# Seven-product first projection for two of six block pairs in token tiles 3 to 6, in the four PSUM banks of the projection's ring

## The chip, the core and the metric

The kernel runs on one core of one Trainium2 chip. The metric is the device time of one execution in microseconds. The engines of the core are called PE (TensorE; PEld is its weight load), DVE (VectorE), ACT (ScalarE), POOL (GpSimd) and SP (SyncE, which only issues transfers here).

## What is computed

Sparse attention over 8 batches, 8 heads, 576 positions and head size 64, followed by a bilinear feed-forward layer over the 4608 tokens. The first four heads see the last 32 positions, the other four see every 32nd position.

```
scores = where(mask, q @ k.T / 8, -1e9);  attn = softmax(scores) @ v
x = attn.transpose(0, 2, 1, 3).reshape(4608, 512)
out = ((x @ w_a) * (x @ w_b)) @ w_out        # 512 -> 1536 -> 512
```

## The kernel before, in words

The work after the start is nine tiles of 512 tokens (t = 0 to 8). A tile is 16 slots that are written out in this order: slots 0 to 11 make one block f of 128 hidden features each (`ffn_ab`, L615), slots 12 to 15 the second projection (`ffn_ys`, L860). A scheduled slot ends with `take(i)`, which puts in the attention steps of a later batch, and with what `do(i, ...)` has put there. All engines follow this written order; nothing is reordered.

**A plain block.** PE multiplies x (bf16, transposed, `xT`) by four 128-row pieces of `wa_sb` into one PSUM bank and by four of `wb_sb` into another (L612): eight products of 128x512. ACT copies the first bank to `a_sb` (L633), DVE multiplies it by the second bank into `pf` (L636). The banks come from `mm_bank` (L598), a ring of four: three of pool "mm" and one of pool "tp". A block takes two. The other four banks belong to the attention: "st" (scores) two, "o" (outputs) two.

**A pair by seven products.** In tiles 7 and 8, where attention is over, `a_pair` (L667) makes two blocks f = 2g and 2g+1 at once: of the two-by-two blocks of w_a and x (two halves of the 512 inputs; two halves of 256 tokens) it forms seven products instead of eight, each two matmuls of 128x256. They are called 1, 6, 7, 2, 5, 4, 3 in its plan (L683). They need sums of weights (`wsum_make`, L648, tiles `wsum_a`) and of inputs (`xsum_make`, L659, tiles `xsum`). Product 1, then 6, then 5 accumulate in bank X, 3 later too, and X is copied out by ACT after each; 7 and 4 accumulate in bank Z; 2 goes to bank Y. DVE adds Y and the second content of Z to the copies, POOL the first content of Z. X, Y and Z lie in three different banks, X in one that the attention has left.

**What else stands in a slot of tiles 3 to 6** (`LATER`, L575, the batch b = t+1). The step after the named slot is, for PE: slot 0 S1, slot 1 V0, slot 2 S2, slot 3 V1, slot 4 S3, slot 5 V2, slot 6 S4, slot 7 V3. S is a score step: PE `st` (L377), ACT exp (L397), DVE mask (L415). V0 to V3 are output steps: PE `o` (L454), DVE reciprocal `rc` (L462) and multiplication `xl` (L480). Q2 after slot 1 and Q3 after slot 3 are two POOL copies each (`step_Q`, L333). `fast_s` (L750) makes sums for the second projection on DVE after slots 4 to 10. `pace` (L1054) is a one-element POOL copy of a slot's result that holds POOL's transfers back until that slot; it stands at each slot in which `do` has put something.

In the tables the step "mask" is L415, "rc" L462, "xl" L480, "ps" L750.

Of the kernel before, what the change touches and what calls it, by code (L numbers as in the profile page):

```python
# [7 lines left out]
F32 = mybir.dt.float32  # L8
BF16 = mybir.dt.bfloat16
I16 = mybir.dt.int16  # L10
ALU = mybir.AluOpType
# [5 lines left out]
RS = 8  # L17
NP = 72
GP = 80
# [5 lines left out]
VW = 128  # L25
WCH = (0, 2, 5, 9, 12)
FAST_Y = (1, 2, 3, 4, 5, 6, 7, 8)
FAST_A = {7: (1, 2, 3, 4, 5), 8: (0, 1, 2, 3, 4, 5)}


@with_exitstack
def kernel(
# [10 lines left out]
    nc = tc.nc  # L43
    B, H, S, D = q.shape
# [5 lines left out]
    KD = d_model // 128  # L50
    FD = d_ff // 128
    TTOK = 512
    NT = n_tok // TTOK
# [3 lines left out]
    const = ctx.enter_context(tc.tile_pool(name="const", bufs=1))  # L57
    wp = ctx.enter_context(tc.tile_pool(name="weights", bufs=1))
    nat = ctx.enter_context(tc.tile_pool(name="nat", bufs=1))
    sb = ctx.enter_context(tc.tile_pool(name="sb", bufs=3))  # L60
    fsb = ctx.enter_context(tc.tile_pool(name="ffn", bufs=2))
# [18 lines left out]
    qz_flat = [[l.rearrange("p a b c -> p (a b c)"), s.rearrange("p a b c d -> p (a b c d)")] for l, s in qz_pair]  # L80
# [3 lines left out]
    vl_buf = [const.tile([128, HL * 6, VW], BF16, name=f"vl{i}") for i in range(2)]  # L84
# [75 lines left out]
    XR = 4  # L160
    xT = const.tile([128, KD, XR * S], BF16)
    wa_sb = wp.tile([128, KD, d_ff], BF16)
    wb_sb = wp.tile([128, KD, d_ff], BF16)
    wo_sb = wp.tile([128, FD, d_model], BF16)

    FG = FD // 2
    HT = TTOK // 2
# [9 lines left out]

    tl = {}

    def blocks(nm, z):  # L180
        z = int(z)
        return sb.tile([128, 2, (S, RS * GP)[z]], BF16, tag=f"t{nm}{z}", name=f"t{nm}{z}", bufs=1)


    nats = {}
# [408 lines left out]
    pfs = {}  # L594
# [3 lines left out]
    def mm_bank(shape):  # L598
        nm = "tp" if used[0] % 4 == 3 and used[0] >= 0 else "mm"
        used[0] += 1  # L600
        return psum4[nm].tile(shape, F32, tag=nm, name="mm")
# [13 lines left out]
    def ffn_ab(t, f, mid, ab=None):  # L615
        if f == 0:
            pfs[t] = fsb.tile([128, FD, TTOK], BF16, tag="pf", name="pf", bufs=1)
        pf = pfs[t]
        if f // 2 in FAST_A.get(t, ()):
            if f % 2 == 0:  # L620
                pairs[t, f // 2] = a_pair(t, f // 2)
            return next(pairs[t, f // 2])
        if ab is None:
            ab = [mm_bank([128, TTOK]) for _ in range(2)]
            if f == 0:

                late = 1 if t == 1 else 3
                for kks in ((0, 2, 3), (1,)) if t == 1 else ((0, 2), (1,), (3,)):
                    ab_mm(t, f, ab, kks, last=kks[-1] if kks[-1] == late else -1)
            else:  # L630
                ab_mm(t, f, ab, range(KD), mid)
        a_sb = fsb.tile([128, TTOK], F32, tag="a_sb", name="a_sb")
        nc.scalar.copy(a_sb, ab[0])  # L633
        if t in FAST_Y:
            halves = lambda x: x.rearrange("p (a i s) -> p a i s", i=2, s=16)
            nc.vector.tensor_mul(pf[:, f, :].rearrange("p (i a s) -> p a i s", i=2, s=16), halves(a_sb), halves(ab[1]))  # L636
        else:
            nc.vector.tensor_mul(pf[:, f, :], a_sb, ab[1])
        return pf[:1, f, :1]

    wav = wa_sb.rearrange("p (j c) (g e m) -> p j c g e m", c=2, e=2, m=128)
    wsum_a = [flat.rearrange("p (c g m) -> p c g m", c=2, g=FG)
              for flat in [vl_buf[0].rearrange("p a b -> p (a b)")[:, 12 * 128 * z:12 * 128 * (z + 1)] for z in range(2)]
              + [t[:, :12 * 128] for t in qz_flat[0]]]
    xsum = {t: qz_flat[1][t - 7][:, :8 * HT].rearrange("p (n c m) -> p n c m", n=4, c=2)
            for t in FAST_A}

    def wsum_make(n):  # L648
        w, s_ = (lambda e, j: wav[:, j, :, :, e]), wsum_a
        a, b, op = ((w(1, 0), w(1, 1), ALU.add), (s_[0], w(0, 0), ALU.subtract), (w(0, 0), w(1, 0), ALU.subtract),  # L650
                    (w(0, 1), s_[1], ALU.subtract))[n]
        for c in range(2):
            nc.vector.tensor_tensor(s_[n][:, c], a[:, c], b[:, c], op=op)

    def x_part(t, j, k):
        x0 = TTOK * t % (XR * S) + HT * k
        return xT[:, 2 * j:2 * j + 2, x0:x0 + HT]

    def xsum_make(t, n):  # L659
# [4 lines left out]

    pairs = {}

    def a_pair(t, g):  # L667

        pf = pfs[t]
        pool, nm = ((pst, "st"), (psum4["o"], "o"))[g % 2]  # L670
        X = pool.tile([128, 2, 512], F32, tag=nm, name="ax")[:, 0, :HT]
        a = ([fsb.tile([128, TTOK], F32, tag="a_sb", name="a_sb") for _ in range(2)] if g % 2 == 0 else
             [t.rearrange("p h n -> p (h n)")[:, :2 * TTOK].bitcast(F32) for t in kT_buf[0]])
        got = {k: psum4[nm].tile([128, TTOK], F32, tag=nm, name="mm")
               for k, nm in zip((1, "Z", "Y", 0), (("mm", "mm", "tp", "mm"), ("tp", "mm", "mm", "mm"))[g % 2])}
        Z, Y = got["Z"][:, :HT], got["Y"][:, :HT]
        p7 = fsb.tile([128, HT], F32, tag="p7", name="p7")
        quarter = lambda e, k: a[e][:, HT * k:HT * (k + 1)]
        w = lambda e, j: (lambda c: wav[:, j, c, g, e])
        ws = lambda n: (lambda c: wsum_a[n][:, c, g])  # L680
        x = lambda j, k: (lambda c: x_part(t, j, k)[:, c])
        xs = lambda n: (lambda c: xsum[t][:, n, c])
        plan = {"1": (X, w(0, 0), x(0, 0)), "2": (Y, w(0, 1), x(1, 0)), "3": (X, ws(3), x(1, 1)), "4": (Z, w(1, 1), xs(3)),  # L683
                "5": (X, ws(0), xs(0)), "6": (X, ws(1), xs(1)), "7": (Z, ws(2), xs(2))}

        def P(k):
            bank, lhs, rhs = plan[k]
            for c in range(2):
                nc.tensor.matmul(bank, lhsT=lhs(c), rhs=rhs(c), start=k in "172" and c == 0, stop=c == 1, skip_group_check=True)  # L689

        x0 = TTOK * t % (XR * S)

        def b_mm(e, kks):
            f = 2 * g + e
            for kk in kks:
                nc.tensor.matmul(got[e], lhsT=wb_sb[:, kk, 128 * f:128 * (f + 1)], rhs=xT[:, kk, x0:x0 + TTOK],  # L696
                                 start=kk == 0, stop=kk == KD - 1)

        def mult(e):
            halves = lambda v_: v_.rearrange("p (a i s) -> p a i s", i=2, s=16)  # L700
            nc.vector.tensor_mul(pf[:, 2 * g + e, :].rearrange("p (i a s) -> p a i s", i=2, s=16),
                                 halves(a[e]), halves(got[e]))

        P("1")
        nc.scalar.copy(quarter(0, 0), X)
        b_mm(1, (0, 1, 2))
        P("6")
        nc.scalar.copy(quarter(1, 0), X)
        b_mm(1, (3,))
        P("7")  # L710
        nc.scalar.copy(p7, Z)
        P("2")
        nc.vector.tensor_tensor(quarter(0, 0), Y, quarter(0, 0), op=ALU.add)
        yield None
        P("5")
        nc.scalar.copy(quarter(1, 1), X)
        nc.gpsimd.tensor_tensor(quarter(1, 1), quarter(1, 1), p7, op=ALU.add)
        if (t, g - 1) in later:
            later.pop((t, g - 1))()
        b_mm(0, (0, 1))  # L720
        P("4")
        nc.vector.tensor_tensor(quarter(1, 0), Z, quarter(1, 0), op=ALU.add)
        P("3")
        nc.scalar.copy(quarter(0, 1), X)
        b_mm(0, (2, 3))
        if g < FG - 1:
            mult(1)
            mult(0)
        else:
            mult(0)  # L730
            if t < NT - 1:
                fast_s(t, 2, slice(4, 6))
            mult(1)
        yield pf[:1, 2 * g + 1, :1]
# [172 lines left out]
    with tc.manual_schedule(engines={ENG.PE, ENG.SP, ENG.Pool, ENG.DVE, ENG.Activation}):  # L907
# [30 lines left out]
        for nm in ORDER:  # L938
            if nm[0] == "*":
                spin(int(nm[1:]))  # L940
            elif nm == "C0":
                for x, cp, n in ((raw[0], nc.vector.tensor_copy, "k"), (raw[1], nc.scalar.copy, "q")):
                    t = nats[0, n, False][:, 0:2].rearrange("p h r d -> p (h r d)")
# [21 lines left out]
            elif nm[0] == "F":  # L965
                f = int(nm[1])
# [6 lines left out]
                elif nm == "F0B":  # L973
                    first[f].append(psum4["o"].tile([128, 512], F32, tag="o", name="ab"))
                ab_mm(0, f, first[f], {"A": (0, 1), "B": (0, 1), "b": (2,), "c": (3,)}[nm[2]],
                      ws={"A": (0,), "B": (1,)}.get(nm[2], (0, 1)))
# [5 lines left out]
        for t in range(NT):  # L982
            slots += [(ffn_ab, t, f) for f in range(FD)] + [(ffn_ys if t in FAST_Y else ffn_y, t, j) for j in range(4)]
        for b in range(1, B):
# [8 lines left out]
        def do(i, fn, *args):  # L993
            at.setdefault(i, []).append(lambda: fn(*args))

        soon = {}
        for t in FAST_Y[:-1]:
            if t not in FAST_A:
# [21 lines left out]
            for (z, nm), g in zip(((0, "k"), (0, "q"), (1, "k"), (1, "q")), gs):  # L1020
                do(g0 + g, step_D, b, z, nm)
        for n in range(4):
            do(16 * (NT - 3) + 2 * n + 2, wsum_make, n)
        do(16 * (NT - 2) - 1, xsum_make, NT - 2, 0)
        for n in (2, 1, 3):
            do(16 * (NT - 2), xsum_make, NT - 2, n)
# [11 lines left out]
        for g in range(FG):  # L1038
            for n in range(4):
                do(16 * (NT - 1) + 2 * g + 1, fast_s, NT - 1, n, slice(g, g + 1))  # L1040
        for t in FAST_Y[:-1]:
            for slot, n, z0, z1 in ((4, 0, 0, 2), (5, 2, 0, 2), (6, 1, 0, 2), (7, 3, 0, 2), (8, 2, 2, 4), (9, 0, 2, 4),
# [45 lines left out]
```

## Time and profile before

| what | value |
|---|---|
| three timed runs | 326.03, 326.70, 327.37 us (median 326.7) |
| the profiled execution | 326.64 us; its span is 324.9 us |
| granted TensorE clock | 0.997 |
| PE busy | 315.5 us, 97% of the span |
| DVE, ACT, POOL busy | 234.1, 186.4, 150.1 us |
| tile 3 / 4 / 5 / 6, first product of slot 0 | 127.97 / 161.64 / 195.55 / 229.22 us |

Times in the profile are counted from the start of the span. A row of the timeline gives start, duration, engine, source line, operation, destination and sources, and in brackets how long the engine was idle before and for whom. A matmul row of four products of 128x512 lasts 1.03 us to the last value in PSUM, but the next one starts 0.862 us after it, since matmuls overlap; spacing is therefore taken from starts. The same holds for DVE rows that follow each other.

### The profile page before, as it was taken

What the parts mean: (1) busy time and instruction counts of PE and PEld (TensorE: products, weight loads), DVE (VectorE), ACT (ScalarE), POOL (GpSimd) and SP (SyncE); (2) the same over time, 40 slices, a digit from 0 to 9 for tenths busy, and PEclk for the clock granted to TensorE, in tenths of its full rate; (3) what the DMA queues carried; (4) which work ended last, traced back from release to release, by engine and by line L of the source; (5) the groups of instructions that cost most, each with busy time, mean ns of one, the idle gap of its engine ahead of it and who ended that gap; (6) DMA issues with size and microseconds to landing.
All of it is one profiled execution on the core that took longest, in us unless ns stands there. A gap on an engine that the chain in (4) does not pass through costs nothing.

```text
span 324.9 us, 7111 instructions
## 1 busy us (share of the span) xinstructions
PE 315.5 (97%) x2706; PEld 214.2 (66%) x2734; DVE 234.1 (72%) x489; ACT 186.4 (57%) x331; POOL 150.1 (46%) x240
## 2 busy tenths in 40 slices
PE   8999999998999999999999999999999999999994
PEld 6754555454765578556999995559555866786684
DVE  6765786498956785688667766777699667857862
ACT  6763766454754476447644765467546655535541
POOL 8944922893785356524652565336124003202520
PEclk9999999999999999999999999999999999999998
DMA  8999999999699999999998999999863030004004
GB/s 150 155 204 196 204 187 204 204 126 175 87 132 153 191 129 101 131 207 167 102 104 181 158 107 107 158 182 112 59 101 103 2 113 17 3 2 129 0 3 129
DMA packets 127234, 40.40 MB, mean 124 GB/s; under 512 B 115040, under 2 KB 124320, under 8 KB 127008
## 3 DMA queue, kind: packets, MB, share of 16 engines
q0 software_dynamic: 80400, 19.28, 64.5%
q1 hardware_dynamic: 46656, 20.61, 36.3%
q8 instruction: 21, 0.34, 0.5%
q14 instruction: 13, 0.11, 0.1%
q10 hardware_dynamic: 144, 0.07, 0.1%
HBM read 39.12 MB, written 18.28 MB: 177 GB/s over the span
## 4 chain that ended last, share of the span: by engine, by line
PE 89%; DVE 4%; ACT 2%; issue 2%; DMA 2%; POOL 0%; ACTq 0%; POOLq 0%
PE mm L612 42%; PE mm L816 18%; PE mm L696 5%; PE st L377 4%; PE mm L878 3%; PE ax L689 3%; PE o L454 2%; PE mm L689 2%; PE o L513 2%; DMA shared<-in_q_dram 2%; PE mm L843 2%; PE end L843 1%; DVE p L415 1%; PE misc L156 1%; PE tp L540 1%
## 5 line engine op out<-in xcount | busy, mean ns | idle before, releaser
L612 PE MATMUL mm<-xT,wb_sb 128*128 128x512 bf16 (+1 forms) x381 | 88.0, 352 | 0.4
L612 PE MATMUL mm<-xT,wa_sb 128*128 128x512 bf16 (+1 forms) x367 | 86.6, 351 | 0.6
L633 ACT COPY a_sb<-mm 128x512 f32<-128x512 f32 x84 | 49.2, 585 | 47.1 <-PE mm L612 45.5
L636 DVE TENSOR_TENSOR pf<-a_sb,mm 128x512 bf16<-128x512 f32 x74 | 50.6, 684 | 26.0 <-PE mm L612 18.4
L612 PEld LDWEIGHTS <-wb_sb 128*128 128x128 bf16 x392 | 37.8, 98 | 33.7 <-issue 0.4
L1054 POOL CAST pace<-pf 1x1 f32<-1x1 bf16 x72 | 21.0, 291 | 77.0 <-DVE pf L636 47.8
L612 PEld LDWEIGHTS <-wa_sb 128*128 128x128 bf16 x392 | 34.9, 98 | 20.9
L397 ACT ACTIVATE p<-st 72x576 bf16<-72x576 f32 (+1 forms) x56 | 36.4, 650 | 20.1 <-PE st L377 19.8
L816 PEld LDWEIGHTS <-ps 128*128 128x128 bf16 x336 | 32.5, 98 | 4.6 <-issue 0.5
L527 DVE TENSOR_TENSOR xT<-o,xr 64x576 bf16<-64x576 f32 x24 | 18.0, 751 | 19.8 <-ACT xr L524 19.6
L816 PE MATMUL mm<-wf,ps 128*128 128x256 bf16 x252 | 30.1, 273 | 0.5 <-ACT y_sb L781 0.3
L781 ACT COPY y_sb<-mm 128x512 f32<-128x512 f32 (+1 forms) x32 | 17.9, 559 | 19.3 <-PE mm L816 16.6
L816 PEld LDWEIGHTS <-pf 128*128 128x128 bf16 x252 | 23.6, 98 | 2.7
L696 PE MATMUL mm<-xT,wb_sb 128*128 128x512 bf16 x83 | 25.3, 379 | 0.1
L816 PE MATMUL mm<-wo_sb,pf 128*128 128x256 bf16 x168 | 21.8, 273 | 0.0
L750 DVE TENSOR_TENSOR ps<-pf 128x512 bf16<-128x512 bf16 (+1 forms) x49 | 21.2, 433 | 0.7
L523 ACT ACTIVATE xr<-o 64x576 f32<-64x576 f32 x24 | 15.6, 648 | 9.4 <-PE o L513 9.2
L1054 POOL COPY pace<-y_sb 1x1 f32<-1x1 f32 x17 | 4.1, 241 | 36.0 <-ACT y_sb L887 13.3
L236 POOL DMA_DIRECT2D vs<-in_v_dram x24 | 20.4, 863 | 0.0
L415 DVE TENSOR_TENSOR p<-p,mask_s 72x576 int16<-72x576 int16 x28 | 18.7, 669 | 1.8 <-ACT p L397 1.5
L454 PEld LDWEIGHTS <-p 128*128 128x128 bf16 (+1 forms) x256 | 13.0, 97 | 8.9 <-DVE xl L480 2.1
L415 DVE TENSOR_TENSOR p<-p,mask_l 128x576 int16<-128x576 int16 x32 | 14.7, 458 | 4.3 <-ACT p L397 4.3
(183 smaller groups left out, 546.7 us busy)
## 6 DMA issues: line engine op xcount, KB each, us to landing
out_dram<-y_sb SPq DMA_DIRECT2D x14, 512.0 KB, 4.9
kr<-in_k_dram POOLq DMA_DIRECT2D x12, 288.0 KB, 5.8
qr<-in_q_dram POOLq DMA_DIRECT2D x12, 288.0 KB, 6.9
vl<-in_v_dram POOLq DMA_DIRECT2D x6, 384.0 KB, 9.5
out_dram<-y_sb SPq DMA_DIRECT2D x7, 256.0 KB, 4.1
vs<-in_v_dram POOLq DMA_DIRECT2D x24, 72.0 KB, 5.9
xd<-xl SPq DMA_DIRECT2D x12, 144.0 KB, 4.8
wo_sb<-in_moe_w_out_dram POOLq DMA_DIRECT2D x4, 384.0 KB, 10.4
```

Of the source, the lines that this page charges most:

```text
L236: nc.gpsimd.dma_start(out=vs_buf[b % 2][:, h, :, 0:D], in_=v[b, HL + h].rearrange("(p r) d -> p r d", r=RS))
L397: nc.scalar.activation(p_flat(p)[:M, :2 * W].rearrange("p (i n) -> p i n", n=2 * n), st[:M].rearrange("p a (i n) -> p (a i) n", n=256)[:, ...
L415: nc.vector.tensor_tensor(pi, pi, mk, op=ALU.bitwise_and)
L454: nc.tensor.matmul(of[:, j, i, :w], lhsT=pt, rhs=vt, start=True, stop=True)
L527: nc.vector.tensor_mul(dst.rearrange("d (p i j) -> d p i j", i=G, j=2), o[:64, :, :W].rearrange("d j (i p) -> d p i j", p=NP), r)
L612: nc.tensor.matmul(ps_[:, c0:c0 + n], lhsT=w[:, kk, 128 * f:128 * (f + 1)], rhs=xT[:, kk, x0:x0 + n], start=(kk == first and c0 == 0), sto ...
L633: nc.scalar.copy(a_sb, ab[0])
L636: nc.vector.tensor_mul(pf[:, f, :].rearrange("p (i a s) -> p a i s", i=2, s=16), halves(a_sb), halves(ab[1]))
L696: nc.tensor.matmul(got[e], lhsT=wb_sb[:, kk, 128 * f:128 * (f + 1)], rhs=xT[:, kk, x0:x0 + TTOK], start=kk == 0, stop=kk == KD - 1)
L750: nc.vector.tensor_tensor(s[:, n], a, b, op=op)
L816: nc.tensor.matmul(bank[b][:, q], lhsT=lhs(g, q), rhs=rhs(g), start=k in "172" and q == 0 and g == 0, stop=g == FG - 1, skip_group_check=True)
L1054: nc.gpsimd.tensor_copy(pace, done)
```

## The change

- A table `MID_A` names pairs g = 1 and g = 3 (slots 2 and 3, slots 6 and 7) of tiles 3, 4, 5 and 6. They are made by a new function, `a_pair_mid`, instead of as two plain blocks each.
- `a_pair_mid` takes four banks of the ring: X, b1, b0 and one bank YZ, whose first half is Y and whose second half is Z.
- The weights' sums move from the tile before 7 to tile 2 (slots 3, 7, 9 and 13), and lie in staging tiles of the first two batches, which are made larger for this. Each mid tile gets four `xsum_make`: one at the last slot of the tile before, three after its slot 0. They share one buffer, `xsum_mid`.
- `a_sb` has three buffers instead of two.

```diff
+MID_A = {t: (1, 3) for t in (3, 4, 5, 6)}
...
-        if f // 2 in FAST_A.get(t, ()):
+        if f // 2 in FAST_A.get(t, ()) + MID_A.get(t, ()):
             if f % 2 == 0:
-                pairs[t, f // 2] = a_pair(t, f // 2)
+                pairs[t, f // 2] = (a_pair_mid if t in MID_A else a_pair)(t, f // 2)
             return next(pairs[t, f // 2])
...
+    def a_pair_mid(t, g):
...
+        YZ, X, b1, b0 = [mm_bank([128, TTOK]) for _ in range(4)]
+        X, Y, Z = X[:, :HT], YZ[:, :HT], YZ[:, HT:]
+        a = [fsb.tile([128, TTOK], F32, tag="a_sb", name="a_sb", bufs=3) for _ in range(2)]
...
+        P(X, w(0, 0), x(0, 0), True)
+        nc.scalar.copy(quarter(0, 0), X)
+        P(Y, w(0, 1), x(1, 0), True)
+        add(quarter(0, 0), Y)
+        b_mm(b1, 1, (0, 1, 2))
+        P(X, ws(1), xs(1))
+        nc.scalar.copy(quarter(1, 0), X)
+        P(Z, ws(2), xs(2))
+        b_mm(b1, 1, (3,))
+        P(X, ws(0), xs(0))
+        nc.scalar.copy(quarter(1, 1), X)
+        add(quarter(1, 1), Z)
+        yield a[1][:1, HT:HT + 1]
+        b_mm(b0, 0, (0, 1, 2))
+        P(Z, w(1, 1), xs(3))
+        add(quarter(1, 0), Z)
+        b_mm(b0, 0, (3,))
+        P(X, ws(3), x(1, 1))
+        nc.scalar.copy(quarter(0, 1), X)
+        mult(1, b1)
+        mult(0, b0)
+        yield pf[:1, 2 * g, :1]
...
         for n in range(4):
-            do(16 * (NT - 3) + 2 * n + 2, wsum_make, n)
+            do(16 * 2 + (3, 7, 9, 13)[n], wsum_make, n)
+        for t in MID_A:
+            do(16 * t - 1, xsum_make, t, 0)
+            for n in (1, 2, 3):
+                do(16 * t, xsum_make, t, n)
```

`P` is two matmuls of 128x256 into the named half bank, `add` a DVE addition of a half bank to a quarter of `a_sb`, `mult` the multiplication of L701, `b_mm` products of 128x512 with `wb_sb`. By the numbers of `a_pair` the order is 1, 2, 6, 7, 5, then (after the slot's attention step) 4, 3. With the waits that the built program carries, product 7 waits for the addition of Y, product 4 for the addition of Z, products 6, 5 and 3 for the copy of X before them, and the next block's two banks for the last addition of Z and the last copy of X.

## The prediction

> **What bounds the kernel now.** I read the page's first part, then the busy times by stretch (tiles 3, 4 and 5: length, then busy us of PE, PEld, DVE, ACT, POOL), then the timeline of tile 5 and of a pair of tile 7.
>
> ```profile
> PE 315.5 (97%) x2706; PEld 214.2 (66%) x2734; DVE 234.1 (72%) x489; ACT 186.4 (57%) x331; POOL 150.1 (46%) x240
> ```
>
> ```profile
> 128.00:161.60 33.60, 33.44 (x263) 21.35 (x264) 24.43 (x47) 20.12 (x34) 16.85 (x28) 1.00 1.33 156
> 161.60:195.50 33.90, 33.90 (x363) 30.76 (x361) 24.48 (x47) 20.18 (x33) 17.48 (x28) 1.00 1.14 135
> 195.50:229.20 33.70, 33.54 (x264) 21.44 (x265) 24.52 (x47) 20.22 (x34) 15.78 (x26) 1.00 1.38 137
> ```
>
> PE is never idle in the tiles that change, so every matmul removed there is worth its full spacing, and every wait put on PE costs its full length. DVE has room on average (24.5 of 33.7 us). What counts is when DVE is free. Tile 5 around the start of slot 2:
>
> ```profile
> 198.39 1.03 PE L612 MATMUL mm<-xT,wb_sb 128*128 128x512 bf16 x4
> 198.49 0.45 DVE L415 TENSOR_TENSOR p<-p,mask_l 128x576 int16<-128x576 int16 x1
> ...
> 199.20 1.32 POOL L333 COPY qz0s<-qTs 64x576 bf16<-64x576 bf16 x2 [1.34 <-DMA qTs<-qr]
> 199.25 0.35 PE L454 MATMUL o<-vl,p 128*128 128x65 bf16 x6
> 199.44 1.02 PE L612 MATMUL mm<-xT,wa_sb 128*128 128x512 bf16 x4
> 199.53 0.69 DVE L636 TENSOR_TENSOR pf<-a_sb,mm 128x512 bf16<-128x512 f32 x1 [0.59 <-PE mm L612]
> 200.13 0.18 DVE L462 RECIPROCAL rc<-o 96x6 f32<-96x6 f32 x1
> 200.30 1.03 PE L612 MATMUL mm<-xT,wb_sb 128*128 128x512 bf16 x4
> 200.35 0.55 DVE L480 TENSOR_TENSOR xl<-o,rc 96x384 bf16<-96x384 f32 x1
> ```
>
> When PE starts slot 2 (199.44), DVE has just begun the block before (mult, 199.53) and has rc and xl of V0 behind it. Four products of 128x512 take 199.44 to 200.30 on PE, 0.2155 each. The two-matmul products of tile 7 show the other spacings and releases:
>
> ```profile
> 266.97 0.38 PE L689 MATMUL ax<-qz1l,vl 128*128 128x256 bf16 x2
> ...
> 267.39 0.37 ACT L708 COPY kT0s<-ax 128x256 f32<-128x256 f32 x1 [0.49 <-PE ax L689]
> ...
> 268.49 0.38 PE L689 MATMUL mm<-qz1l,wa_sb 128*128 128x256 bf16 x2
> ...
> 268.98 0.42 DVE L722 TENSOR_TENSOR kT0s<-mm,kT0s 128x256 f32<-128x256 f32 x1 [0.44 <-PE mm L689]
> ```
>
> A product's first matmul to its ACT copy is 0.42, the copy 0.37; to its DVE addition 0.49, the addition 0.425. Pairs start at 269.36 and 272.61 there: 3.25 us without a wait.
>
> **The change, part by part.**
>
> *Matmuls.* A pair of plain blocks is 16 x 0.2155 = 3.45 us of PE, the new one 3.25: 0.20 saved, 8 x 0.20 = **1.6 us**.
>
> *Product 7 waits for the addition of Y.* Y and Z share a bank, so 7 may start only when DVE has read Y. In `a_pair` they lie apart, and no row of before shows this wait; it is worked out from rows. Let T be the start of the pair. Products 1, 2, three of b1 and 6 take 3 x 0.218 + 0.647 = 1.30, so PE is at 7 at T+1.30. DVE, in pair g = 1: the mask starts at T-0.95 (198.49) and is out of the way at T-0.54 (mask to next operation 0.41); then come the three new `xsum_make`, spaced 0.38 (the three rows of the same kind in tile 7 fill 265.58 to 266.71), to T+0.59; mult 0.60, rc 0.22, xl 0.47 (208.12 to 208.59), to T+1.88; the addition 0.425, to T+2.31; DVE to PE 0.06 (xl ended at 74.12, the PE row that had waited for it starts at 74.18). Product 7 starts at T+2.36: **1.06 us of PE idle**. In pair g = 3 there is no `xsum_make`, but a `ps` of slot 5: mult starts at T+0.09, the chain 0.60 + 0.22 + 0.47 + 0.38 ends at T+1.76, the addition at T+2.19, product 7 at T+2.25: **0.95**. DVE cannot work ahead: its chain begins with the block that PE has just finished.
>
> The Trainium skill (PSUM — Partial Sum Buffer, "PSUM bank collisions raise a hardware error") says that two engines must not touch one bank in the same partitions at once, whichever columns, so waits go by bank. By address alone the 1.06 and 0.95 would vanish; by bank they stand, and this is how the built program waits.
>
> *Product 4* (Z again) waits for the addition of the first Z, which follows the copy of X after 5: from the start of 5, 0.42 + 0.37 + 0.03 + 0.425 + 0.06 = 1.31, while PE has 0.22 + 0.25 (S) + 0.65 = 1.12 to do: **0.19**. *The next block* takes the bank of Z or of X. From product 4's start PE is there after 0.22 + 0.215 + 0.22 + 0.18 (V) = 0.83. The last addition of Z stands on DVE behind the mask of S2 or S4 (and in g = 3 another `ps`), whose exp follows the copy of 5; it ends after 1.00 (g = 1) or 1.38 (g = 3), plus 0.06: **0.23** and **0.61**. In tiles 4 and 5 the bank taken after g = 3 is X's, free 1.28 after product 4's start: **0.45**. X itself costs nothing: after the wait at 7 the copies are long done.
>
> Sum: g = 1: 1.06 + 0.19 + 0.23 - 0.20 = +1.28, taken four times 5.1; g = 3: +1.55 in tiles 3 and 6, +1.39 in 4 and 5, together 5.9. **+11.0 us.**
>
> *POOL's copies beside the three `xsum_make`.* Q2 runs on POOL from 131.37, 199.20 and 232.97 in tiles 3, 5 and 6, when T is 131.85, 199.44 and 233.10: it overlaps T-0.54 to T+0.59, where the new DVE rows now stand. In tile 4 it ran earlier (162.89), but a new `pace` of slot 0 now stands before it, which ends about T-0.6. What such an overlap does:
>
> ```profile
> 117.46 1.52 DVE L415 TENSOR_TENSOR p<-p,mask_s 72x576 int16<-72x576 int16 x1
> ...
> 117.53 1.14 POOL L335 COPY qz0l<-qTl 64x1152 bf16<-64x1152 bf16 x1
> ```
>
> The mask usually takes 0.46; here it ends 0.3 after POOL. Of twelve DVE rows with two SBUF inputs that lie beside such a copy by more than 0.2 us, ten are held like this (masks, `ps`, `wf`); the rows that read PSUM are not. Bounds per tile: 0, or the two copies, 1.33. Nearest rows say held; I take it for three of four tiles: **+4.0**. The Trainium skill (SBUF — State Buffer, "SBUF: two separate sides") has the rule: a DVE operation with two SBUF inputs and a POOL operation that reads SBUF exclude each other for the whole instruction, and whichever starts first wins. By it POOL would lose where `xsum_make` is first; then the sum is +11.0. The row above speaks against that half: DVE's start is stamped first and DVE was held.
>
> *The rest.* ACT gains four copies of 0.37 for two of 0.59 per pair, 0.3 us, beside PE's waits. Four `xsum_make` per tile are counted where they stand; the first lies in the last slot, where DVE was idle 1.0 us before its row at 194.93. `wsum_make` moves eight operations of 0.55 to tile 2. Most fall into DVE's idle time, but two stand before the sums of the second projection, whose fourth block needs DVE at 121.08 and has it at 120.83; bounds 0 and 0.8, I take 0, since a POOL copy held DVE there already until 118.98. In tile 6 they leave DVE time that PE never waited for: 0. New `pace` copies on POOL (0.17 each) wait for slots that are over when POOL comes; behind them stand Q2 and loads with several us to spare: 0. The third `a_sb` buffer: 0.
>
> Sum: 326.64 + 11.0 + 4.0 = **341.7 us**. The median of the timed runs, 326.7, is the profiled time within 0.1, so nothing is to be corrected.
>
> **Rivals.**
> 1. *Bank waits, but DVE is not held by POOL* (or in one tile at most): 326.6 + 11.0 = 337.7, to 339.0. For it: the mask at 164.59 beside a POOL copy was not held. 0.24.
> 2. *DVE arrives earlier*, about half the wait: 328.5 to 336.5. It needs shorter spacing of DVE's rows than any seen, or PE late for another reason. 0.10.
> 3. *The other side: the saving survives.* The addition of Y would have to end by T+1.25, that is, stand ahead of mult, rc and xl on DVE, where its own input comes 0.71 after T (0.218 + 0.49). Then 7 and the next bank cost nothing and product 4 at most 0.19: 326.6 - 1.6 = 325.0, with 0.19 eight times 326.5. Against it: DVE works in written order and the addition is written behind V0 or V2. 0.03 for a gain, 0.02 for no change.
> 4. *More than this*, all four tiles held and tile 2 late too: 326.6 + 11.0 + 5.3 + 0.8 = 343.7, and beyond 344.5 if further DVE rows are held. 0.03 beyond.
>
> **How the numbers follow.** Forecast (held in two to four tiles, 339.0 to 344.5): 0.58; rival 1: 0.24; the others as above. The range 336.5 to 344.5 takes in the forecast and rival 1, 0.82; its lower end leaves 1.2 for the small waits of 0.19 and 0.23, which are the least sure. Faster by over 0.5% (1.6 us, about what a measurement of this kernel can tell from no change): 0.03, within 0.5%: 0.02, slower: 0.95.
>
> **What the profile after would show.** PE idle some 1 us before product 7 in every mid pair, released by the addition on DVE, nearer 2.3 us in g = 1 where DVE was held; smaller gaps before product 4 and the next block; `xsum_make` rows after slot 0 of 1 us and more instead of 0.42 beside POOL's Q2. Tiles 3 to 6 should be 36.5 to 38 us long instead of 33.7, tiles 7 and 8 as before. No idle PE before product 7 would make the prediction wrong at its root; gaps of 1 us in both pairs would make rival 1 right.

## The result and the profile after

The changed kernel takes **342.82 us** (median of five runs, 342.74 to 343.24) against 326.58 us of the kernel before (five runs beside them): ratio 1.0501, 95% interval 1.0485 to 1.0517. The prediction was 341.7, range 336.5 to 344.5. Here and below, the ratios and the time of run 10 leave out executions that took over 1.5% longer than the fastest of the same kernel (in run 10 one of 1165.85 us). The profiled execution of the new kernel takes 343.24 us, its span is 341.5 us, 16.6 more than the span before.

PE is hardly busier (320.6 us against 315.5), and stands idle instead. The first row is the page's busy time of PE; the table by stretch gives tiles 3 and 5 (length, then busy us of PE, PEld, DVE, ACT, POOL, then the granted clock):

```profile
PE 320.6 (94%) x2766; PEld 217.4 (64%) x2766; DVE 251.7 (74%) x529; ACT 187.9 (55%) x347; POOL 151.4 (44%) x247
```

```profile
129.13:167.69 38.56, 35.67 (x279) 23.27 (x278) 28.97 (x57) 20.71 (x38) 18.01 (x30) 0.96 1.12 127
...
205.03:242.20 37.17, 34.23 (x279) 22.63 (x277) 28.91 (x57) 20.59 (x38) 16.85 (x29) 1.00 1.11 128
```

By the first product of each tile, tile 2 is 0.75 us longer than before, tiles 3 to 6 are 4.89, 3.43, 3.50 and 3.47 longer, tiles 7 and 8 are as before (0.0 and 0.17). PE's waits, summed (total us, times, longest), name the place, the addition L705 of `a_pair_mid`, ahead of L684, the matmuls of the products:

```profile
PE mm L684 <- DVE a_sb L705: 10.4, 8, 1.9
...
PE mm L879 <- DVE ps L813: 0.7, 2, 0.6
PE mm L617 <- ACT a_sb L725: 0.6, 2, 0.3
PE mm L617 <- DVE a_sb L705: 0.5, 2, 0.3
```

Tile 5 around the start of the second pair, the place of the excerpt of before (rows of one timeline, T = 208.91):

```profile
208.33 1.68 DVE L670 TENSOR_TENSOR xsum<-xT,xsum 128x512 bf16<-128x512 bf16 x1
208.39 1.32 POOL L338 COPY qz0s<-qTs 64x576 bf16<-64x576 bf16 x2
...
208.91 0.60 PE L684 MATMUL mm<-xT,wa_sb 128*128 128x256 bf16 x4
...
210.60 0.67 DVE L641 TENSOR_TENSOR pf<-a_sb,mm 128x512 bf16<-128x512 f32 x1
211.19 0.18 DVE L467 RECIPROCAL rc<-o 96x6 f32<-96x6 f32 x1
211.41 0.55 DVE L485 TENSOR_TENSOR xl<-o,rc 96x384 bf16<-96x384 f32 x1
211.88 0.41 DVE L705 TENSOR_TENSOR a_sb<-mm,a_sb 128x256 f32<-128x256 f32 x1
212.35 0.38 PE L684 MATMUL mm<-xsum,tk 128*128 128x256 bf16 x2 [1.89 <-DVE a_sb L705]
```

Read it along DVE: three sums (the first held to 1.68 beside POOL's copies, the others, not shown, at 209.93 and 210.26), mult, rc, xl, and only then the addition of Y, whose input had been ready since about 209.7 (ACT's copy of product 1 ended then). Product 7 (212.35) comes 2.06 after PE could have started it; the bracket says 1.89, because it counts from the modelled end of the row before, while the spacing counts from starts. By spacing, the waits of the four tiles agree within 0.03 (two of those in tile 3 can't be read, since they lie in the slow stretch told below): in g = 1 0.06 to 0.08 before product 6, for a held sum, 2.06 before product 7 (1.90 once in run 3), 0.18 to 0.19 before product 4, 0.09 at the next block; in g = 3 0.88, 0.18 and 0.41 to 0.44.

### The profile page after: what moved, and what is told of

The parts are those of the page before. It is cut to its first block, busy times and chain, and to the rows that moved or that the text cites. A ratio compares the mean times of both kernels' runs of the same rounds, so it can differ in the third digit from the quotient of the medians.

```text
span 341.5 us, 7258 instructions
## 1 busy us (share of the span) xinstructions
PE 320.6 (94%) x2766; PEld 217.4 (64%) x2766; DVE 251.7 (74%) x529; ACT 187.9 (55%) x347; POOL 151.4 (44%) x247
## 4 chain that ended last, share of the span: by engine, by line
PE 73%; DVE 11%; DMA 4%; POOL 4%; issue 3%; ACT 3%; DVEq 0%; POOLq 0%; ACTq 0%
PE mm L617 28%; PE mm L879 16%; PE mm L759 5%; DMA wb_sb<-in_moe_w_b_dram 4%; PE st L382 3%; DVE pf L641 3%; PE mm L941 3%; PE ax L752 3%; PE mm L684 3%; DVE xsum L670 2%; PE mm L697 2%; PE mm L752 2%; PE o L518 2%; DVE p L420 2%; PE mm L906 2%
## 5 line engine op out<-in xcount | busy, mean ns | idle before, releaser
L617 PE MATMUL mm<-xT,wa_sb 128*128 128x512 bf16 (+1 forms) x304 | 72.0, 356 | 1.1 <-ACT a_sb L725 0.6
L617 PE MATMUL mm<-xT,wb_sb 128*128 128x512 bf16 (+1 forms) x304 | 72.0, 357 | 0.0
L638 ACT COPY a_sb<-mm 128x512 f32<-128x512 f32 x68 | 39.7, 584 | 32.0 <-PE mm L617 31.8
L1121 POOL CAST pace<-pf 1x1 f32<-1x1 bf16 x68 | 17.6, 259 | 75.6 <-DVE pf L641 42.5
L641 DVE TENSOR_TENSOR pf<-a_sb,mm 128x512 bf16<-128x512 f32 x58 | 39.5, 681 | 13.2 <-PE mm L617 6.8
L617 PEld LDWEIGHTS <-wb_sb 128*128 128x128 bf16 x312 | 30.0, 98 | 27.9 <-DMA wb_sb<-in_moe_w_b_dram 0.5
L617 PEld LDWEIGHTS <-wa_sb 128*128 128x128 bf16 x312 | 28.3, 98 | 19.3 <-issue 1.4
L759 PE MATMUL mm<-xT,wb_sb 128*128 128x512 bf16 x88 | 26.2, 379 | 0.0
L1121 POOL COPY pace<-y_sb 1x1 f32<-1x1 f32 x21 | 7.6, 360 | 38.2 <-ACT y_sb L950 13.6
L697 PE MATMUL mm<-xT,wb_sb 128*128 128x512 bf16 (+1 forms) x80 | 20.1, 350 | 0.0
L705 DVE TENSOR_TENSOR a_sb<-mm,a_sb 128x256 f32<-128x256 f32 x24 | 10.0, 418 | 11.6 <-ACT a_sb L717 11.0
```

The costliest lines, as they stand in the source:

```text
L617: nc.tensor.matmul(ps_[:, c0:c0 + n], lhsT=w[:, kk, 128 * f:128 * (f + 1)], rhs=xT[:, kk, x0:x0 + n], start=(kk == first and c0 == 0), sto ...
L697: nc.tensor.matmul(dst, lhsT=wb_sb[:, kk, 128 * f:128 * (f + 1)], rhs=rhs, start=kk == 0 and k in (None, 0), stop=kk == KD - 1 and k in (N ...
L1121: nc.gpsimd.tensor_copy(pace, done)
```

## The experiments

Tile lengths below are from each run's trace; before has 33.67, 33.91, 33.67, 33.43 for tiles 3 to 6. Tiles 0 to 2 vary by up to 1.5 us from one execution to the next with the arrival of transfers, so that tile lengths tell more than single times.

**1. Everything but the products.**

```diff
-MID_A = {t: (1, 3) for t in (3, 4, 5, 6)}
+MID_A = {t: () for t in (3, 4, 5, 6)}
```

> No tile uses the seven products in a mid pair, everything else of the change stays: the sums of weights in tile 2, the sums of tokens (made in tiles 3 to 6, never read), the third a_sb buffer, the pace copies. Theory (the cost is the shared bank of Y and Z, which makes PE wait for a DVE that is late): without the shared bank the late DVE costs PE nothing, so only tile 2's 0.75 us stays, 326.6 + 0.75 = 327.3. Rival (the work added to DVE and POOL costs by itself, by holding the next blocks' banks): the three sums, held by POOL's copies, put DVE 2 us late once in each of four tiles, 327.3 + 4 to 8 = 331 to 335.

Measured 327.63 us, ratio 1.0029 (1.0009 to 1.0049). Tiles 3 to 6 are 33.67, 33.91, 33.67, 33.43, exactly as before, and tile 2 is 34.44, 0.77 longer. The sums are held just as in the change:

```profile
198.81 1.67 DVE L670 TENSOR_TENSOR xsum<-xT,xsum 128x512 bf16<-128x512 bf16 x1
198.87 1.32 POOL L338 COPY qz0s<-qTs 64x576 bf16<-64x576 bf16 x2
...
199.39 1.02 PE L617 MATMUL mm<-xT,wa_sb 128*128 128x512 bf16 x4
...
201.07 0.67 DVE L641 TENSOR_TENSOR pf<-a_sb,mm 128x512 bf16<-128x512 f32 x1
```

DVE starts mult 201.07 - 199.39 = 1.68 after slot 2 began, against 0.09 before the change, and PE never waits for it. So a late DVE alone costs nothing; it is the pair, whose product 7 waits for the bank that Y shares, that turns it into time. The rival of this run falls. (The run takes out the whole pair; none of the runs gives Y and Z a bank each.)

**2 and 3. One pair alone.** `(3,)` and `(1,)` in place of `(1, 3)`.

> Only the fourth block pair uses the seven products, in tiles 3 to 6. Theory: each such pair is 1.31 us longer by the trace of after (0.88 before product 7, 0.18 before product 4, 0.41 to 0.44 at the next block, 0.20 saved), and the held sums before the second pair cost nothing since that pair has no shared bank: 326.6 + 0.75 (tile 2) + 4 x 1.31 = 332.6. Rival (each pair's waits feed the next): more than 334, or less than 331.

> Only the second block pair uses the seven products, in tiles 3 to 6. Theory: each such pair is 2.21 us longer by the trace of after (2.06 before product 7, 0.19 before product 4, 0.09 at the next block, some 0.20 saved): 326.6 + 0.75 + 4 x 2.21 = 336.2, and 1.4 more, 337.6, if TensorE's clock drops in tile 3 after the idle time before product 7 as it did in after. Rival: the two pairs' costs do not add up, so that this and the fourth pair alone give together a good deal more or less than after (this below 334 or above 339).

Measured 332.91 us, ratio 1.0191 (1.0154 to 1.0228), tiles 1.26 to 1.30 longer; and 337.35 us, ratio 1.0364 (1.0283 to 1.0444), tiles 3.61, 2.17, 1.97 and 2.21 longer, the first with the clock drop told below, both close to what was expected (332.6 and 337.6). The parts add up: 327.63 + (332.91 - 327.63) + (337.35 - 327.63) = 342.6 against 342.8.

**4. The sums of tokens earlier.**

```diff
-                do(16 * t, xsum_make, t, n)
+                do(16 * t - 1, xsum_make, t, n)
```

> The change with the three sums of tokens made in the slot before the tile instead of after slot 0, so that they lie beside none of POOL's copies and not ahead of slot 1's mult on DVE. Theory: in g = 1 product 7 then waits only for mult, rc, xl and the addition, T+0.09 + 0.60 + 0.22 + 0.47 + 0.43 + 0.06 = T+1.87 against T+1.30, 0.57 instead of 2.06: 4 x 1.5 = 6.0 less, and without an idle time of 2 us the half clock in tile 3 (1.4) goes too: 342.8 - 7.4 = 335.4 (336.8 if the clock still drops). Rival (POOL does not hold them; only their own 1.15 us count): 342.8 - 4 x 1.15 = 338.2 at best. Rival (the wait at product 7 has another cause than DVE's backlog): 342.8.

Measured 339.71 us, ratio 1.0393 (1.0338 to 1.0449): a miss, and no test of the hold. With nothing put at slot 0, no pace copy stands there, and POOL's Q2 starts earlier too, beside the sums again (tile 5, T = 208.99):

```profile
206.66 2.57 POOL L338 COPY qz0s<-qTs 64x576 bf16<-64x576 bf16 x2
...
207.05 0.81 DVE L670 TENSOR_TENSOR xsum<-xT,xsum 128x512 bf16<-128x512 bf16 x1
...
209.45 0.67 DVE L641 TENSOR_TENSOR pf<-a_sb,mm 128x512 bf16<-128x512 f32 x1
...
210.18 0.38 PE L684 MATMUL mm<-xT,wa_sb 128*128 128x256 bf16 x2 [0.81 <-DVE pf L641]
```

Here the copies and the sums (the two not shown take 0.91 each) slow each other, and slot 0's mult (209.45) is so late that even its bank is missed: product 2 waits 0.81 for it (in tile 3 product 1 waits, 2.01 by spacing). Product 7 still waits 0.69 to 0.91 in tiles 3 to 5. Only in tile 6 did the two miss each other, and there product 7 waits 0.55, as expected (0.57); its tile is 1.6 shorter than in the change (35.31 against 36.90).

**5. POOL's copies later, the sums where they are.**

```diff
+            do(16 * t + 1, lambda: None)
```

(nothing but a pace copy after slot 1, behind which Q2 stands)

> The change with one more pace copy on POOL after slot 1 of tiles 3 to 6, so that POOL's Q2 copies start when slot 1 is multiplied, beside rows of DVE that read PSUM, and not beside the three sums of tokens. Nothing else moves. Theory: the sums then take 0.38 each, and product 7 in g = 1 waits for DVE's chain alone, 1.06 instead of 2.06: 342.8 - 4 x 1.0 = 338.8, and 337.4 if the half clock in tile 3 goes with the shorter idle time. Rival (the hold is not what makes the sums long): 342.8. Rival (the copies now hold another row, the mask of slot 2, and the wait comes back before product 4): 339.5 to 342.

Measured 336.37 us, ratio 1.0287 (1.0213 to 1.0362); tiles 2.15 to 2.24 longer instead of 3.43 to 4.89. The sums take 0.42 each, DVE's queue ahead of the addition is otherwise the same (tile 5, PE at product 7 0.88 late):

```profile
203.29 0.42 DVE L670 TENSOR_TENSOR xsum<-xT,xsum 128x512 bf16<-128x512 bf16 x1
203.62 0.42 DVE L670 TENSOR_TENSOR xsum<-xT 128x512 bf16<-128x512 bf16 x1
...
204.29 0.68 DVE L641 TENSOR_TENSOR pf<-a_sb,mm 128x512 bf16<-128x512 f32 x1
...
205.59 0.41 DVE L705 TENSOR_TENSOR a_sb<-mm,a_sb 128x256 f32<-128x256 f32 x1
```

So the hold is worth 2.06 - 0.88 = 1.18 before product 7 (1.21 in tile 4, where 0.85 is left), and 1.26 to 1.28 per tile where the clock had held, with the 0.07 before product 6. TensorE's clock stays at 1.00.

**6 and 7. The products in another order, without and with that gate.** In short (X1 is product 1 into X):

```diff
 X1, copy
-Y2, add Y
 b1 (0,1,2);  X6, copy
-Z7;  b1 (3);  X5, copy, add Z
+Z7, ACT copy to p7;  b1 (3);  X5, DVE adds X and p7
 yield
+Y2, add Y
 b0 (0,1,2);  Z4, add Z;  b0 (3);  X3, copy
```

> The change with the order of the products turned: 1, b1, 6, 7, b1, 5, then 2 (Y), b0, 4, 3. Product 7 is read off by ACT into p7 and enters through the addition after 5, so that Y's addition is wanted by PE only at product 4, 0.87 after product 2. POOL's copies stay as they are and still hold the sums. Theory: in g = 3 DVE is through with rc and xl by T+1.76, and the addition of Y ends 0.1 after PE wants product 4, so 0.3 is left of 1.31 with the next block's 0.4; in g = 1 the held chain ends at T+2.9, two additions behind it at T+3.8, where PE wants product 4 at T+2.85: 0.85 left of 2.21. 326.6 + 0.75 + 4 x (0.3 + 0.85) = 332.0. Rival (DVE's backlog costs PE the same in any order): 340 to 342.8.

> The turned order and the POOL copies after slot 1 together. Theory: nothing is late in g = 1 (0.1 before product 4 and 0.1 at the next block against 0.2 saved), 0.3 is left in g = 3 by the next block's wait: 326.6 + 0.75 + 4 x 0.3 = 328.6. Rival (one of the two alone already gives all): equal to the better of the two.

Measured 337.21 us, ratio 1.0291 (1.0229 to 1.0353), and 336.46 us, ratio 1.0275 (1.0202 to 1.0348). Both expectations failed, and for one reason. The addition of Y now stands behind the `yield`, and so behind the mask of the attention step that is put in there (tile 5 of run 7):

```profile
206.77 0.42 DVE L717 TENSOR_TENSOR a_sb<-mm,p 128x256 f32<-128x256 f32 x1 [0.40 <-PE mm L684]
...
207.63 0.46 DVE L420 TENSOR_TENSOR p<-p,mask_l 128x576 int16<-128x576 int16 x1 [0.44 <-ACT p L402]
...
208.01 0.42 DVE L705 TENSOR_TENSOR a_sb<-mm,a_sb 128x256 f32<-128x256 f32 x1
...
208.48 0.38 PE L684 MATMUL mm<-xsum,wa_sb 128*128 128x256 bf16 x2 [0.70 <-DVE a_sb L705]
```

DVE is idle for 0.44 with Y ready, since the mask ahead of the addition waits for its exp on ACT. The wait at product 7 is gone and 0.86 (g = 1) and 1.19 (g = 3, with a `ps` too) stand before product 4. That wait is the same with the sums held or not; the gate only takes away 0.29 to 0.31 per tile, most of which product 6 waits in run 6 for a held sum itself (tiles of 36.11, 36.28, 36.10, 35.87 without it, 35.81, 35.98, 35.81, 35.56 with it). So run 7 ends where its rival put it, at the better of the two single changes (336.37 in run 5). It is the same mechanism in a new place: what matters is what stands ahead of the addition in DVE's written order.

**8. All mends, product 3 ahead of 4, X in the oldest bank, weights' sums in other slots.**

> The turned order and the POOL copies after slot 1, with product 3 ahead of product 4 and X in the oldest bank (so that the next block takes a bank that ACT frees early), and the sums of weights in slots 1 and 2 of tile 1 and 0 and 2 of tile 2, where DVE has idle time. Theory: no wait is left in the mid pairs or in tile 2, and the matmuls' saving of 8 x 0.2 survives: 326.6 - 1.6 = 325.0, faster than before by 0.5%. Rival (the additions that DVE gains put it late somewhere else, or the sums of weights cost their 0.75 in the new place as well): 326 to 328.

Measured 332.29 us, ratio 1.0146 (1.0099 to 1.0192); tiles 34.82, 35.00, 34.83, 34.58, longer than before by 1.09 to 1.16. The mask is still ahead of the addition: 0.43 and 0.76 before product 4, which now comes 0.43 later on PE. 0.19 stands before product 5, for ACT's copy after 6, as in run 7. The next block no longer waits.

**9. Y ahead of the mask.** Against run 8, in the same short form:

```diff
 b1 (3)
+b0 (0)
 X5, DVE adds X and p7
-yield
 Y2, add Y
-b0 (0,1,2)
+yield
+b0 (1,2)
 X3, copy;  b0 (3);  Z4, add Z
```

and the weights' sums after slots 0 to 3 of tile 2.

> As the run before with all mends, but product 2 and the addition of Y stand ahead of the next attention step, so that DVE does not stand in that step's mask (which waits for its exp on ACT) when Y is ready; one matmul of b0 is moved ahead of product 5, so that ACT's copy after product 6 is through; the sums of weights in slots 0 to 3 of tile 2, ahead of the sums of the second projection. Theory: what was left there (0.19 before product 5, 0.43 and 0.76 before product 4) came from these two orders alone, so no wait is left and the saving survives: tiles 3 to 6 of 33.3 us instead of 33.7 before, 326.6 - 1.6 = 325.0. Rival (the chain on DVE is too long for any order, and the wait comes back at the next block): tiles of 34.2 to 34.8, 328 to 331. Rival (the sums of weights still make tile 2 late by 0.75): 325.7.

Measured 325.84 us, ratio 0.9987 (0.9962 to 1.0011). No wait over 0.03 is left in the mid pairs: tiles 3 to 6 are 33.33, 33.52, 33.33 and 33.09, 0.34 to 0.39 shorter than before, although DVE has 27.6 us of work in them instead of 24.5. The mask now stands behind the addition, and its wait for the exp holds back nothing that product 4 needs (tile 5):

```profile
200.19 0.41 DVE L705 TENSOR_TENSOR a_sb<-mm,a_sb 128x256 f32<-128x256 f32 x1
...
200.94 0.38 PE L684 MATMUL mm<-xsum,wa_sb 128*128 128x256 bf16 x2
200.96 0.46 DVE L420 TENSOR_TENSOR p<-p,mask_l 128x576 int16<-128x576 int16 x1 [0.35 <-ACT p L402]
```

The gain is there in the trace, but the interval does not tell it from nothing. The same kernel on its own again:

> The version without waits once more, on its own, since its interval against before (0.9962 to 1.0011) did not tell 0.5% from nothing. Theory: the saving seen in the trace (tiles 3 to 6 shorter by 0.34 each, 1.4 us in all) is there in every execution: ratio 0.9957. Rival (the shorter tiles are given back before or after them): ratio 1.000, and a span that is not shorter though tiles 3 to 6 are.

325.75 us, ratio 0.9984 (0.9958 to 1.0011), tiles 3 to 6 the same to 0.01. In this execution tile 2 took 34.59: two of the weights' sums were held to 2.06 and 2.08 by POOL's copies, and PE waited 0.76 for a mult behind them.

**10. V0 one slot later** (on top of run 5).

```diff
-1: "V0 Q2", 2: "S2",
+1: "Q2", 2: "V0 S2",
```

> The change with POOL's Q2 after slot 1, as in the run with that alone, and with V0 moved from slot 1 to slot 2 (in all later tiles), so that rc and xl no longer stand ahead of the addition of Y in g = 1; g = 3 is left as it is. Theory: the wait at product 7 is DVE's queue ahead of the addition; without rc and xl it ends by T+1.27, where PE is at T+1.30, so 0.88 of g = 1 vanishes and 0.88 of g = 3 stays: 3.5 less than that run (span 333.95 - 3.5 = 330.4). Rival (the wait is not that queue, or V0's rows are late for slot 2 and come back before product 4): no less than that run, or g = 3 changed too.

Measured 335.46 us, ratio 1.0287 (1.0248 to 1.0326), the ratio of run 5: the 3.5 us less that were expected did not come. In g = 1 the wait before product 7 falls from 0.88 to 0.37 (0.34 in one tile), in g = 3 it stays at 0.88: taking rc and xl from DVE's queue shortens this wait and no other. That it is not zero was a mistake in the expectation, which left out the three sums; mult starts at T+0.61 in this run's tile 5, and the chain gives 0.61 + 0.60 + 0.41 + 0.06 = T+1.68 against T+1.30, the 0.37 seen. The wait falls by 0.5 and not by the 0.7 of rc and xl, since V0's matmuls on PE (0.18) no longer stand ahead of the pair either. And rc and xl are now ahead of the last additions, so the next block waits 0.39 to 0.50 instead of 0.09; 0.2 to 0.35 per tile is left of the gain, in the trace.

**12. The weights' sum of slot 9 after slot 5 instead**, the rest as in run 9.

```diff
-            do(16 * 2 + n, wsum_make, n)
+            do(16 * 2 + (3, 7, 5, 13)[n], wsum_make, n)
```

> The version without waits in the mid pairs, with the sums of weights where the change has them (slots 3, 7, 9, 13 of tile 2), except that the one of slot 9 is made after slot 5. Theory: of the four only the one after slot 9 made tile 2 late, since it stands right ahead of the sums of the second projection (0.75 in six runs); one after slot 3 may be held by POOL's copies, as in the change, and costs nothing. Tile 2 takes 33.7, tiles 3 to 6 33.3, and the time is 326.6 - 1.4 = 325.2, ratio 0.9957. Rival (any of them in tile 2 costs it, as in one execution with slots 0 to 3): tile 2 of 34.4 or more, and no difference from the two runs before.

Measured **325.53 us, ratio 0.9953 (0.9927 to 0.998)**: here the interval lies just below 1. Part of that is the kernel before, whose median beside this run was 327.34 us, against 326.64 and 326.51 beside runs 9 and 11. The kernel's own three medians (325.84, 325.75, 325.53) lie within 0.3 us, so that the times of the three runs put the gain at 0.1 to 0.5%, two of them with intervals that take in no gain at all. Tile 2 has no wait for DVE any more; its 34.13 are 33.67 and 0.46 for a transfer in its first slot. Tile 3:

```profile
127.51:160.83 33.32, 33.32 (x278) 22.58 (x277) 27.60 (x57) 20.60 (x38) 17.80 (x31) 1.00 1.21 132
```

PE is never idle, as before the change, and tiles 3 to 6 are each 0.34 to 0.39 shorter, 1.4 us in all, in the traces of runs 9, 11 and 12 alike.

## Why the prediction was right, point by point

| step | predicted | measured |
|---|---|---|
| matmuls saved per pair | 0.20 | 0.17 to 0.20 (runs 9 and 12: 0.34 to 0.39 per tile) |
| wait before product 7, g = 1, not held | 1.06 | 0.85 to 0.88 (run 5) |
| the same, g = 3 | 0.95 | 0.88 |
| hold by POOL's copies | 1.33 in three tiles of four | 1.18 to 1.21 in all four (after against run 5) |
| before product 4 | 0.19 | 0.18 to 0.19 |
| next block, g = 1 / g = 3 | 0.23 / 0.61 and 0.45 | 0.09 / 0.41 to 0.44 |
| weights' sums in tile 2 | 0, at most 0.8 | 0.75 |
| granted clock | not thought of | 1.4, in tile 3 of the profiled execution |

The mechanism was right: the bank that Y and Z share, DVE's written order, POOL's copies on top. Runs 1, 5 and 10 show the three parts separately: without the shared bank a DVE late by 1.6 us costs nothing, without the copies 1.18 goes, without rc and xl 0.5 goes. That it is the bank is shown by the wait itself: product 7 does not use the result of the addition of Y, and PE waits for that addition. The sum came out 1.1 too low (1.5 for the profiled execution), and errors of both signs met in it, so that it came this close is in part luck. Of the four tiles 3.75 each had been forecast on average ((11.0 + 4.0) / 4), and 3.43 to 3.50 were found where the clock held, 1.1 less in all. Missing were, in the profiled execution, tile 2 (0.75), the clock in tile 3 (4.89 - 3.47 = 1.4) and 0.65 ahead of the first product of tile 0, which differs by as much between executions of other kernels here.

The wait before product 7 was over-sized because DVE's rows follow each other a little closer than taken: in run 5 the sums are 0.33 apart (203.29, 203.62, 203.96), not 0.38, and mult starts at 204.29, T+0.42 instead of T+0.59. The waits of the next block were over-sized because the last addition of Z ends 0.87 (g = 1) and 1.19 (g = 3) after the start of product 4 in tile 5 of the change, not 1.00 and 1.38.

That the sums would be held had less behind it than the prediction says. In the rows of before, not twelve but sixteen DVE rows with two SBUF inputs lie beside one of POOL's Q copies by more than 0.2 us. Ten are held; the other six (162.76 and 164.59, and the `ps` rows at 120.41, 154.07, 187.94 and 221.66) keep their usual length, and there POOL's copy is the longer one (1.36 instead of 1.14 beside a `ps`; 2.71 instead of 1.32 for two beside the masks). That the sums are held in all four tiles is known from the runs alone.

The step that failed is "a POOL copy held DVE there already", the cover for the weights' sums, which put tile 2 at 0; it cost 0.75. In tile 2 the sum made after slot 9 stands at the head of a queue that is not idle again until the mask is held once more:

```profile
116.48 1.01 DVE L660 TENSOR_TENSOR tk<-wa_sb 128x768 bf16<-128x768 bf16 x2
117.41 0.41 DVE L813 TENSOR_TENSOR ps<-pf 128x512 bf16<-128x512 bf16 x1
...
118.80 1.52 DVE L420 TENSOR_TENSOR p<-p,mask_s 72x576 int16<-72x576 int16 x1
...
122.23 1.05 PE L879 MATMUL mm<-wf,ps 128*128 128x256 bf16 x8 [0.58 <-DVE ps L813]
```

The hold does not replace the added work, it moves along behind it: the mask was merely held later (118.80 instead of 117.46, of which 0.41 is the later start of the tile). Run 12 moves that one sum, and the wait is gone.

Rival 3, that the saving survives, was given 0.05. Its condition, that Y is read by the time PE needs the bank again, was named rightly. The way that it gave (the addition ahead of mult, rc and xl) is in none of the runs; runs 9 and 12 meet the condition by an order in which PE needs the bank later, and there the saving does survive in tiles 3 to 6.

## What to carry to other kernels

When two results of a product share a PSUM bank, ask not how long the read takes but what is written ahead of that read in the reading engine's queue; an engine that may be 1.6 us late at no cost becomes the bound as soon as the producer needs its bank back within that time. Place such a read ahead of anything that waits for a third engine (here a mask behind an exp), and leave a distance on the producer that covers matmul, read and queue. A saving of 0.17 to 0.20 per pair shows in the time only when the waits are gone: six of these twelve runs had the same matmuls and were slower than before.

## What the runs showed of the hardware

**The clock.** In the profiled execution of the change TensorE's granted clock fell to half after the wait in tile 3 (stretches of one table; the clock is the column after POOL's):

```profile
134.18:136.46 2.28, 0.39 (x3) 0.20 (x3) 2.19 (x6) 0.37 (x1) 0.00 (x0) 1.00 1.60 102
136.46:136.74 0.28, 0.28 (x2) 0.21 (x2) 0.00 (x0) 0.00 (x0) 0.00 (x0) 0.74 0.31 20
136.74:139.78 3.04, 3.04 (x12) 1.67 (x11) 0.88 (x2) 1.02 (x2) 0.69 (x3) 0.50 0.00 0
```

Matmuls of 128x512 come 0.43 apart there instead of 0.2155, from 136.60 to 140.01, which is 3.41 us, at a cost of 1.4 in this trace. Run 3 shows the same once, also in tile 3 (136.89 to 140.31); the waits of 1.90 to 2.06 in tiles 4 to 6 of both show nothing, nor does one of 2.01 in tile 3 of run 4, and in run 5, whose waits are 0.88, the clock stays at 1.00. The Trainium skill (TensorE: Matmul & The Clock Gate, "Part 1: The HAM clock gate (the "warmup" mystery)") says that activity is watched in free-running windows of about 3.4 us, and that the clock is halved after an idle one. The length of the slow stretch agrees with that; the idle time does not have to fill a window, since some 2.1 us of it were enough here.

The traces say a little more. In each of them the time from the clock's rise to full speed to its next drop is a whole multiple of 3.413 us (in the change 39 such steps up to the drop in tile 3, and 59 from 140.01 to the drop at the program's end). Laid out in these steps, the step that ends with the drop holds 2.13 us of idle PE by spacing, in the change and in run 3 alike: the 2.06 before product 7 and the 0.07 or 0.08 before product 6. The fullest steps without a drop behind them hold 2.06 and 2.05 (run 3, tiles 4 and 6) and 2.01 (run 4, tile 3); the waits of the change in tiles 4 to 6 are cut in two by the end of a step. So a small wait that falls into the same step may have decided. This is read from two drops, and no run tests it.

What the drop adds to the measured time is open. One of the four timed executions without a trace had a mean clock of 0.999, which leaves no room for such a stretch (3.41 us at half clock take 0.005 off the mean over 341 us), and yet its span, 341.0, is no shorter by 1.4 than those of the other three (0.993 and 0.994; 341.1 to 341.5). In run 3, one execution with a mean clock of 0.984 took 341.53 us, the others, with 0.994 and 0.995, 337.02 to 337.47.

**Copies on POOL against DVE rows with two SBUF inputs.** In the change the row stamped first on DVE (208.33) is held until 0.3 after POOL's end (208.39 + 1.32); in run 4 the two take turns, the sums 0.81 to 0.91 instead of 0.42 and the copies 2.57 instead of 1.32. Before the change, a mask stamped 0.07 ahead of a copy was held (117.46), while a `ps` row stamped 0.06 ahead of one kept its 0.42 (120.41) and the copy took 1.36 instead of 1.14. The Trainium skill (SBUF — State Buffer, "SBUF: two separate sides") has an exclusive lock for a whole instruction that the first to start gets; the lock agrees, the order does not follow the stamped starts.
